# A first-layer product in one-pass float32r parts instead of float32, for the first batch of an attention-then-FFN kernel

## The chip, the cores and the metric

The kernel runs on one core of one Trainium2 chip. The metric is device time in microseconds (us), the median of several executions. Engines are named as the profile names them: PE is TensorE's matrix multiplication, PEld its weight load, DVE is VectorE, ACT is ScalarE, POOL is GpSimd, SP is SyncE, which only issues DMAs here.

## The reference

Eight batches of eight heads, 576 tokens each, 64 values per head. Keys and values are first gathered into 32 memory slots per head by a softmax over the tokens; queries attend to the slots; the result is a matrix of 4608 tokens by 512, which passes two layers of 2048 with h·cos(h) between them.

```python
a = exp(phi - max(phi, over tokens)); a = a / (sum(a, over tokens) + 1e-9)
k_m = einsum('bhsm,bhsd->bhmd', a, k)
v_m = einsum('bhsm,bhsd->bhmd', a, v)
attn = softmax(q @ k_m.T / sqrt(64))          # 32 slots per head
x = attn @ v_m                                 # -> 4608 x 512
h = x @ w_in                                   # 512 -> 2048
out = (h * cos(h)) @ w_out                     # 2048 -> 512
```

The drawn q and k are multiplied by 64 and phi by 3.26, so the softmax is steep. w_in and w_out arrive as float64 and are read as pairs of 32-bit words.

## The kernel before, in words

The values' memory is folded into the first layer: since x = attn @ v_m, the kernel computes v_m @ w_in once per batch (256 rows, that is 8 heads of 32 slots, by 2048) and multiplies the attention weights, transposed into `aT` (two groups of 128 rows by 576 tokens), with these folded weights. The 4608 tokens are cut into 12 groups of 384, and each group passes the 2048 inner columns in 16 steps of 128. One batch has 576 tokens, so a pair of batches makes three groups: 384 tokens of the first, 192 of the first and 192 of the second (`regions`), and 384 of the second.

In step (grp, f) of the main loop `gemm1` makes the first-layer product `hp`, `act` and `act_end` make h·cos(h), and `gemm2` adds to the output's three accumulators, four steps later (`LAG`).

**Precision.** From group 1 on, all large products go as three float16 products of high and low parts: folded weights `vw` and attention `aT` each have a high and a low half, the activations `gp` and the second-layer weights `wo` too. Splitting needs power-of-two scales, which come from the largest weight, and this is known only when all weights have been converted from float64. Group 0 runs while the weights are still arriving. So it uses plain float32: `fold_first(j)` makes folded weights of 256 columns into `vf` (float32, one tile for each quarter of 512 columns), `gemm1` multiplies them with `aTf` (float32, the first 384 tokens), and `gemm2` uses float32 too. Each float32 product is recorded as two matmul rows with a weight load each. The remaining 192 tokens of batch 0 belong to group 1: `back` in `attend(0)` splits them to float16 in `aT`, and `split_first(q)` splits each quarter of `vf` into `vw_0_q` at steps 14, 18, 22 and 26 of the loop (steps count from 0; 16 to a group).

**Order.** The main loop is written by hand: `convert_next` takes one converted block of weights per step in group 0 and calls `fold_first` after each block of w_in; in group 1 each step has one `w_out_split` and one `w_in_split`; the attention of the coming batches is spread over the steps by `jobs`; `fold(b, q)` for batch 1 stands at steps 12, 16, 20 and 24. Within it, the framework's scheduler orders each engine's instructions.

**Buffers that matter.** The tag `vw` has 8 buffers of 4 KB per partition, `aT` has 3 of 4.6 KB, `raw0` to `raw2` have 8 KB each and hold the raw weights, then the parts of `w_in_split`. The float16 copy of w_in for batches from 2 on (`w2`) goes, for quarter q, into the place of quarter q - 1 of `w_in_sb`, and for quarter 0 into `raw0`.

Lines that the steps below touch: L395 and L398 to L401 (`back`: transposes, high part on ACT, low part on DVE), L466 and L467 (`split_fold`), L484 and L486 (`fold_first`: product, copy), L513 and L522 (`gemm1`, float32 and float16), L533 and L536 (`act`, one pair for each region), L541 (the sine), L545, L547 and L548 (`act_end` from group 1 on: times u, high part, low part), L188/L189 and L199/L200 (splits of w_out and w_in in group 1), L143 to L152 (conversion from float64).

Of the kernel before, what the change touches and what calls it, by code (L numbers as in the profile page):

```python
# [8 lines left out]

F16 = mybir.dt.float16  # L10
F32 = mybir.dt.float32
I16 = mybir.dt.int16
I32 = mybir.dt.int32
I8 = mybir.dt.int8
# [3 lines left out]
ALU = mybir.AluOpType  # L18
# [4 lines left out]
P = 128  # L23
# [4 lines left out]
NP = H // 2  # L28
NF = DF // P
FS = 512  # L30
NQ = DF // FS
WS = 256
# [13 lines left out]
def attention_then_ffn(ctx: ExitStack, tc: tile.TileContext, phi, phiT, kv, qT, w_in, w_out, eye, out):  # L46
# [148 lines left out]
    def w_in_split(q, c):  # L195
        if c == 0:
            st["parts"] = ld.tile([P, 2, NP, FS], F16, tag=f"raw{1 + q % 2}", name=f"w_in_parts_{q}")
        parts, s, src = st["parts"], st["s", "in"], w_in_sb[:, c, q * FS:(q + 1) * FS]
        nc.scalar.activation(parts[:, 0, c], src, AF.Copy, scale=s)  # L199
        nc.vector.scalar_tensor_tensor(out=parts[:, 1, c], in0=src, scalar=s, in1=parts[:, 0, c],  # L200
                                       op0=ALU.mult, op1=ALU.subtract)
        if c < NP - 1:
            return
        if q == 0:
            w2 = ld.tile([P, NP, 2, FS], F16, tag="raw0", name="w_in_2_0")
        else:
            w2 = w_in_sb[:, :, (q - 1) * FS:q * FS].bitcast(F16).rearrange("p c (o f) -> p c o f", o=2)
        for o in range(2):
            here, there = slice(o * D, (o + 1) * D), slice((1 - o) * D, (2 - o) * D)
            nc.sync.dma_start(out=w2[here, :, o], in_=parts[here, 0])  # L210
            nc.sync.dma_start(out=w2[there, :, o], in_=parts[here, 1])
        st["w2", q] = w2
# [99 lines left out]
    def scales(b):  # L312
        E = wk.tile([P, 1], F32, tag="E", name=f"E_{b}", bufs=3)
        nc.vector.tensor_scalar(out=E, in0=st["ev", b], scalar1=st["e", "in"], scalar2=None, op0=ALU.mult)
        cu = wk.tile([P, 1], F32, tag="cu", name=f"cu_{b}", bufs=3)
        nc.vector.tensor_scalar(out=cu, in0=E, scalar1=2.0 ** -27 / (2.0 * math.pi), scalar2=None, op0=ALU.mult)
        st["E", b], st["cu", b] = E, cu
        if b < 2:
# [18 lines left out]

    def attend(b):
        qt, km = loads.pop(("q", b)), st["km", b]
        flat = wk.tile([P, 4 * S], F16, tag="aT", name=f"aT_{b}", bufs=3)  # L340

        t32 = GT if b == 0 else 0
        if b == 0:
            st["aTf"] = flat[:, 0:4 * GT].bitcast(F32).rearrange("p (g x) -> p g x", g=2)
        aT = flat[:, 4 * t32:].rearrange("p (w g x) -> p w g x", w=2, g=2)
        st["aT", b] = aT
# [43 lines left out]

        def back(i):
            t0, n = BL[i]
            if t0 < t32:
                for g in range(2):
                    nc.vector.transpose(st["aTf"][:, g, t0:t0 + n], at[:, 2 * t0 + g * n:2 * t0 + (g + 1) * n])  # L395
                return
            bk = wk.tile([P, 2, n], F32, tag="back", name=f"back_{b}_{t0}", bufs=4)
            nc.vector.transpose(bk.rearrange("p g x -> p (g x)"), at[:, 2 * t0:2 * (t0 + n)])  # L398
            c = slice(t0 - t32, t0 + n - t32)
            nc.scalar.mul(aT[:, 0, :, c], bk, 2.0 ** 14)  # L400
            nc.vector.scalar_tensor_tensor(out=aT[:, 1, :, c], in0=bk, scalar=2.0 ** 14, in1=aT[:, 0, :, c],  # L401
                                           op0=ALU.mult, op1=ALU.subtract)
# [65 lines left out]
                                       op0=ALU.mult, op1=ALU.subtract)  # L468

    def fold(b, q):  # L470
        vw = wk.tile([P, 2, 2, FS], F16, tag="vw", name=f"vw_{b}_{q}", bufs=8)
        st["vw", b, q] = vw
        for g, pv in enumerate([fold_psum(b, q, g) for g in range(2)]):
            split_fold(b, vw, g, pv)

    def fold_first(j):
        q, r = divmod(j, 2)
        if r == 0:
            st["vf", q] = wk.tile([P, 2, FS], F32, tag="vw", name=f"vf_{q}", bufs=8)
        pv = small_ps(f"pvf_{j}").rearrange("p (g x) -> p g x", g=2)  # L480
        for g in range(2):
            for i in range(2):
                c = 2 * g + i
                nc.tensor.matmul(pv[D * i:D * (i + 1), g], lhsT=st["vm", 0][:, c],  # L484
                                 rhs=w_in_sb[:, c, j * WS:(j + 1) * WS], start=True, stop=True)
        (nc.scalar.copy if j < 2 else nc.any.tensor_copy)(out=st["vf", q][:, :, r * WS:(r + 1) * WS], in_=pv)  # L486

    def split_first(q):
        vw = wk.tile([P, 2, 2, FS], F16, tag="vw", name=f"vw_0_{q}", bufs=8)
        for g in range(2):  # L490
            split_fold(0, vw, g, st["vf", q][:, g])
        st["vw", 0, q] = vw

    def prep(b):
        yield from memory(b)
# [12 lines left out]
    def gemm1(grp, f):  # L508
        hp = ps_h.tile([P, 512], F32, tag="ps_h", name=f"hp_{grp}_{f}")
        q, fo = divmod(f, FS // P)  # L510
        if grp == 0:
            for g in range(2):
                nc.tensor.matmul(hp[:, :GT], lhsT=st["vf", q][:, g, fo * P:(fo + 1) * P], rhs=st["aTf"][:, g],  # L513
                                 start=(g == 0), stop=(g == 1))
            return hp
        for b, t0, c0, n in regions(grp):
            vw, aT = st["vw", b, q], st["aT", b]
            c1 = t0 if b else t0 - GT
            k = 0
            for g in range(2):  # L520
                for wi, ai in ((0, 0), (0, 1), (1, 0)):
                    nc.tensor.matmul(hp[:, c0:c0 + n], lhsT=vw[:, wi, g, fo * P:(fo + 1) * P],  # L522
                                     rhs=aT[:, ai, g, c1:c1 + n], start=(k == 0), stop=(k == 5))
                    k += 1
        return hp

    def act(grp, f, hp, pin=False):
        u = ew.tile([P, GT], F32, tag="u", name=f"u_{grp}_{f}", bufs=3)
        gp = ew.tile([P, GT], F32, tag="gp", name=f"gp_{grp}_{f}", bufs=6)
        ni = gp.bitcast(I32)  # L530
        for b, t0, c0, n in regions(grp):
            c, cu = slice(c0, c0 + n), st["cu", b] if grp else 1.0 / (2.0 * math.pi)
            ins = nc.scalar.activation(ni[:, c], hp[:, c], AF.Copy, scale=cu, bias=0.25)  # L533
            if pin:
                tc.keep_in_program_order(ins)
            nc.vector.scalar_tensor_tensor(out=u[:, c], in0=hp[:, c], scalar=cu, in1=ni[:, c],  # L536
                                           op0=ALU.mult, op1=ALU.subtract)
        return u, gp

    def act_end(grp, f, hp, u, gp):  # L540
        nc.scalar.activation(u, u, AF.Sin, scale=TWO_PI_BELOW, bias=quarter)  # L541
        if grp == 0:
            nc.vector.tensor_tensor(out=gp, in0=hp[:, :GT], in1=u, op=ALU.mult)
            return grp, f, gp
        nc.vector.scalar_tensor_tensor(out=u, in0=hp[:, :GT], scalar=2.0 ** -17, in1=u, op0=ALU.mult, op1=ALU.mult)  # L545
# [143 lines left out]
    for i in range(12 * NF):  # L689
# [7 lines left out]
            w_out_split(f)  # L697
        if NF <= i < 2 * NF:
            w_in_split((i - NF) // 4, i % 4)
        if i % 4 == 2 and 0 <= i - 14 < 4 * NQ:  # L700
            split_first((i - 14) // 4)
        hp = gemm1(grp, f)
        last = len(pending) == LAG and pending[0][1] == NF - 1
        if last:
# [71 lines left out]
```

## Time and profile before

| | |
|---|---|
| median of 3 runs | 712.89 us (711.32 to 714.12) |
| the profiled execution | 714.09 us, its span 712.3 us |
| mean granted TensorE clock | 0.988 |
| PE busy, whole span | 686.4 us |
| DVE / ACT busy, whole span | 532.4 / 518.7 us |
| first layer of group 0 (L513) | 64 float32 rows, 28.5 to 107.4 us |
| first layer from group 1 on (L522) | 1440 float16 rows, 110.6 to 696.3 us |

The span runs from the first to the last instruction on any engine; the time of an execution adds a little around it. Busy time is the union of an engine's instructions. Matmuls are pipelined: a row lasts longer than the distance to the next, so that distance, and not the row's length, is what a product costs in a sequence. A row of the chain of waits gives a start, a length and the work (engine, tile, line, count) that held up what came after. In a row of groups, "x8 | 5.8, 748 | 3.0 <-ACT" means eight instructions, 5.8 us busy, 748 ns each, and 3.0 us in which the engine stood idle before them, mostly until that ACT instruction was done.

### The profile page before, as it was taken

The numbers are of one execution on the slowest core, as the hardware profiler recorded it, in microseconds if no ns is written. First come the engines' busy times: TensorE is split into PE (matmuls) and PEld (weight loads), VectorE is DVE, ScalarE is ACT, GpSimd is POOL, SyncE is SP. The second block draws the span as 40 slices with busy tenths as digits, with TensorE's granted clock in tenths as the row PEclk, the third lists the DMA queues.
The fourth block names the chain that finished last, engine by engine and source line by source line (L and its number), as shares of the span: only waits on it lengthen the run. The fifth ranks groups of instructions, "written<-read, shape, count | busy, mean of one in ns | idle before, by whom it ended". The sixth has DMA issues, their size and how long they took to land.

```text
span 712.3 us, 11782 instructions
## 1 busy us (share of the span) xinstructions
PE 686.4 (96%) x4578; PEld 364.3 (51%) x4578; DVE 532.4 (75%) x1132; ACT 518.7 (73%) x951; POOL 13.7 (2%) x34
## 2 busy tenths in 40 slices
PE   7689899999999999999999899999999999999997
PEld 3344345556545445566445445666445454665453
DVE  2869879999968966599667885689567976575552
ACT  1799999898875865778766875678767885665652
POOL 0000000000000000000000100000000000000000
PEclk9799999999999999999999999999999999999999
DMA  8996792325507100170104200151100010100101
GB/s 297 379 333 215 237 320 61 104 60 153 186 1 219 60 1 1 46 235 1 44 1 159 84 37 1 46 179 56 44 2 1 9 37 1 46 1 1 45 0 45
DMA packets 32231, 66.77 MB, mean 94 GB/s; under 512 B 2224, under 2 KB 12336, under 8 KB 32176
## 3 DMA queue, kind: packets, MB, share of 16 engines
q1 hardware_dynamic: 27712, 58.02, 25.1%
q10 hardware_dynamic: 4464, 8.00, 2.9%
q8 instruction: 36, 0.59, 0.4%
q14 instruction: 19, 0.16, 0.1%
HBM read 52.38 MB, written 9.44 MB: 87 GB/s over the span
## 4 chain that ended last, share of the span: by engine, by line
PE 63%; DVE 18%; ACT 15%; DMA 2%; issue 1%; SPq 0%; ACTq 0%; DVEq 0%
PE acc L566 35%; PE hp L522 17%; DVE u L536 3%; ACT u L541 3%; DVE u L545 3%; DVE gp L548 2%; PE psA L258 2%; PE hp L513 2%; PE sc L365 2%; DVE vw L467 2%; PE pv L460 2%; ACT gp L547 2%; DVE wo L189 2%; DMA kv<-in_kv 1%; DVE w_in_parts L200 1%
## 5 line engine op out<-in xcount | busy, mean ns | idle before, releaser
L566 PE MATMUL acc<-wo,gp 128*128 128x512 f16 x1584 | 371.9, 379 | 1.4 <-DVE ob L578 0.7
L566 PEld LDWEIGHTS <-gp 128*128 128x128 f16 x1584 | 153.3, 98 | 162.8 <-issue 4.4
L522 PE MATMUL hp<-aT,vw 128*128 128x192 f16 (+1 forms) x1440 | 202.7, 284 | 1.1 <-DVE u L545 1.1
L522 PEld LDWEIGHTS <-vw 128*128 128x128 f16 x1440 | 128.3, 98 | 77.6 <-issue 17.9
L541 ACT ACTIVATE u<-u,quarter 128x384 f32<-128x384 f32 x192 | 117.0, 616 | 64.5 <-DVE u L536 63.6
L545 DVE SCALAR_TENSOR_TENSOR u<-hp,u 128x384 f32<-128x384 f32 x176 | 96.6, 554 | 60.6 <-ACT u L541 60.1
L533 ACT ACTIVATE gp<-hp,cu 128x192 int32<-128x192 f32 (+1 forms) x240 | 115.3, 492 | 27.9 <-PE hp L522 11.8
L536 DVE SCALAR_TENSOR_TENSOR u<-hp,cu,gp 128x192 f32<-128x192 f32 (+1 forms) x240 | 119.0, 504 | 21.9 <-ACT gp L533 21.5
L547 ACT CAST gp<-u 128x384 f16<-128x384 f32 x176 | 88.9, 510 | 55.2 <-DVE u L545 53.9
L548 DVE TENSOR_TENSOR gp<-u,gp 128x384 f16<-128x384 f32 x176 | 96.5, 553 | 43.0 <-ACT gp L547 41.9
L561 PE MATMUL acc<-wo,gp 128*128 128x512 f32 x96 | 45.1, 599 | 0.0
L513 PE MATMUL hp<-aT,vf 128*128 128x384 f32 x64 | 28.2, 579 | 7.3 <-DVE vf L486 3.1
L467 DVE SCALAR_TENSOR_TENSOR vw<-pv,vw 128x512 f16<-128x512 f32 x48 | 31.5, 685 | 3.0 <-ACT vw L466 2.9
L466 ACT ACTIVATE vw<-pv 128x512 f16<-128x512 f32 x48 | 26.8, 588 | 1.1 <-PE pv L460 0.9
L561 PEld LDWEIGHTS acc<-wo,gp 128*128 128x128 f32 x96 | 17.4, 190 | 17.8 <-issue 15.2
L590 ACT ACTIVATE ob<-acc,os 128x512 f32<-128x512 f32 x27 | 17.8, 682 | 9.7 <-PE acc L566 7.1
L258 PE MATMUL psA<-kv,phi 128*32 128x129 f32 (+1 forms) x640 | 21.0, 275 | 3.2 <-DMA kv<-in_kv 1.8
L513 PEld LDWEIGHTS hp<-aT,vf 128*128 128x128 f32 x64 | 13.3, 220 | 20.9 <-issue 5.9
L541 ACT ACT_TABLE_LOAD x17 | 21.8, 1283 | 0.3
L365 PE MATMUL sc<-q,km 128*64 128x256 f32 (+3 forms) x192 | 19.8, 342 | 2.1 <-DVE vw L467 1.7
L258 PEld LDWEIGHTS psA<-kv,phi 128*32 128x32 f32 (+1 forms) x640 | 16.4, 109 | 9.5 <-issue 3.7
L365 PEld LDWEIGHTS sc<-q,km 128*64 128x64 f32 x192 | 12.1, 140 | 12.6 <-issue 4.4
(130 smaller groups left out, 539.7 us busy)
## 6 DMA issues: line engine op xcount, KB each, us to landing
kv<-in_kv SPq DMA_DIRECT2D x32, 516.0 KB, 7.0
raw_out<-in_w_out SPq DMA_DIRECT2D x8, 1024.0 KB, 6.3
q<-in_qT SPq DMA_DIRECT2D x7, 1152.0 KB, 5.5
out<-ob ACTq DMA_DIRECT2D x30, 256.0 KB, 2.1
raw_in<-in_w_in SPq DMA_DIRECT2D x6, 1024.0 KB, 7.6
phi<-in_phi SPq DMA_DIRECT2D x8, 512.0 KB, 6.1
w_in_sb<-w_in_parts SPq DMA_DIRECT2D x12, 256.0 KB, 4.5
phiT<-in_phiT SPq DMA_DIRECT2D x4, 576.0 KB, 9.4
```

The costliest lines, as they stand in the source:

```text
L258: nc.tensor.matmul(psA[32 * j:32 * (j + 1), g * KV:(g + 1) * KV], lhsT=a[:n, c, h * M:(h + 1) * M], rhs=kvs[c][:n, h * KV:(h + 1) * KV], s ...
L365: nc.tensor.matmul(sc[D * p:D * (p + 1), g * n:(g + 1) * n], lhsT=km[:, 2 * g + p], rhs=qt[:, 2 * g + p, t0:t0 + n], start=True, stop=True)
L513: nc.tensor.matmul(hp[:, :GT], lhsT=st["vf", q][:, g, fo * P:(fo + 1) * P], rhs=st["aTf"][:, g], start=(g == 0), stop=(g == 1))
L522: nc.tensor.matmul(hp[:, c0:c0 + n], lhsT=vw[:, wi, g, fo * P:(fo + 1) * P], rhs=aT[:, ai, g, c1:c1 + n], start=(k == 0), stop=(k == 5))
L533: ins = nc.scalar.activation(ni[:, c], hp[:, c], AF.Copy, scale=cu, bias=0.25)
L536: nc.vector.scalar_tensor_tensor(out=u[:, c], in0=hp[:, c], scalar=cu, in1=ni[:, c], op0=ALU.mult, op1=ALU.subtract)
L541: nc.scalar.activation(u, u, AF.Sin, scale=TWO_PI_BELOW, bias=quarter)
L545: nc.vector.scalar_tensor_tensor(out=u, in0=hp[:, :GT], scalar=2.0 ** -17, in1=u, op0=ALU.mult, op1=ALU.mult)
L547: nc.scalar.copy(gp[:, 0], u)
L548: nc.vector.tensor_tensor(out=gp[:, 1], in0=u, in1=gp[:, 0], op=ALU.subtract)
L561: nc.tensor.matmul(accs[grp][t], lhsT=gp[:, t * P:(t + 1) * P], rhs=wo[:, f + 1], start=(f == 0), stop=(f == NF - 1))
L566: nc.tensor.matmul(accs[grp][t], lhsT=gp[:, gi, t * P:(t + 1) * P], rhs=parts[:, wi], start=(f == 0 and gi == 0 and wi == 0), stop=(f == N ...
```

## The change

Batch 0's first layer, in group 0 and in its half of group 1, is made of three products of float32r parts: high times high, low times high, high times low. A float32r tile is written by an engine with float32r as its output type; the low part is the float32 value less that.

```diff
 def back(i):                                   # in attend(b)
-    if t0 < t32:
+    bk = wk.tile([P, 2, n], F32, tag="back", name=f"back_{b}_{t0}", bufs=4)
+    c = slice(t0, t0 + n)
+    if b == 0:
         for g in range(2):
-            nc.vector.transpose(st["aTf"][:, g, t0:t0 + n], at[:, 2 * t0 + g * n:2 * t0 + (g + 1) * n])
+            nc.vector.transpose(bk[:, g], at[:, 2 * t0 + g * n:2 * t0 + (g + 1) * n])
+            nc.scalar.copy(aTr[0][:, g, c], bk[:, g])
+        nc.vector.tensor_tensor(out=aTr[1][:, :, c], in0=bk, in1=aTr[0][:, :, c].bitcast(F32),
+                                op=ALU.subtract)
         return
...
 def fold_first(j):
-        st["vf", q] = wk.tile([P, 2, FS], F32, tag="vw", name=f"vf_{q}", bufs=8)
+        st["vr", q] = [wk.tile([P, 2, FS], F32R, tag="vw", name=f"vr_{q}_{w}", bufs=8) for w in range(2)]
...
-    (nc.scalar.copy if j < 2 else nc.any.tensor_copy)(out=st["vf", q][:, :, r * WS:(r + 1) * WS], in_=pv)
+    high, low = (t[:, :, r * WS:(r + 1) * WS] for t in st["vr", q])
+    nc.scalar.copy(high, pv)
+    nc.vector.tensor_tensor(out=low, in0=pv, in1=high.bitcast(F32), op=ALU.subtract)
-
-def split_first(q):
-    vw = wk.tile([P, 2, 2, FS], F16, tag="vw", name=f"vw_0_{q}", bufs=8)
-    for g in range(2):
-        split_fold(0, vw, g, st["vf", q][:, g])
-    st["vw", 0, q] = vw
...
 def gemm1(grp, f):
-    if grp == 0:
-        for g in range(2):
-            nc.tensor.matmul(hp[:, :GT], lhsT=st["vf", q][:, g, fo * P:(fo + 1) * P], rhs=st["aTf"][:, g],
-                             start=(g == 0), stop=(g == 1))
-        return hp
     for b, t0, c0, n in regions(grp):
+        if b == 0:
+            k = 0
+            for wi, ai in ((0, 0), (1, 0), (0, 1)):
+                for g in range(2):
+                    nc.tensor.matmul(hp[:, c0:c0 + n], lhsT=st["vr", q][wi][:, g, fo * P:(fo + 1) * P],
+                                     rhs=st["aTr"][ai][:, g, t0:t0 + n], start=(k == 0), stop=(k == 5))
+                    k += 1
+            continue
...
 def act_end(grp, f, hp, u, gp):
-    nc.vector.scalar_tensor_tensor(out=u, in0=hp[:, :GT], scalar=2.0 ** -17, in1=u, op0=ALU.mult, op1=ALU.mult)
+    for b, t0, c0, n in [(1, 0, 0, GT)] if grp > 1 else regions(1):
+        c = slice(c0, c0 + n)
+        nc.vector.scalar_tensor_tensor(out=u[:, c], in0=hp[:, c], scalar=2.0 ** -17 if b else st["G"],
+                                       in1=u[:, c], op0=ALU.mult, op1=ALU.mult)
```

What follows from it: batch 0's part of group 1 is no longer scaled to float16's range, so its half of L545 multiplies by a scale `G` of its own, and `act` uses a constant for it. The eight `vr` tiles fill all eight `vw` buffers, so batch 1's first two quarters of folded weights (`vw_1`, 8 KB) move to `raw0`, and the `w2` copy of quarter q now goes into quarter q of `w_in_sb` itself. `aTr` takes two of the three `aT` buffers. The loop no longer calls `split_first`.

More of the change, by code (lines that the diff above doesn't have):

```diff
@@ L11 @@
 F32 = mybir.dt.float32
+F32R = mybir.dt.float32r
 I16 = mybir.dt.int16
@@ L203, in w_in_split @@
             return
[L204 to L207, printed above, removed]
+        w2 = w_in_sb[:, :, q * FS:(q + 1) * FS].bitcast(F16).rearrange("p c (o f) -> p c o f", o=2)
         for o in range(2):
@@ L317, in scales @@
         st["E", b], st["cu", b] = E, cu
-        if b < 2:
+        if b == 0:
+            G = wk.tile([P, 1], F32, tag="G", name="G", bufs=1)
+            nc.vector.reciprocal(out=G, in_=E)
+            nc.vector.tensor_scalar(out=G, in0=G, scalar1=2.0 ** 10, scalar2=None, op0=ALU.mult)
+            st["G"] = G
+        elif b == 1:
             T = wk.tile([P, 1], F32, tag="T", name=f"T_{b}")
@@ L339, in attend @@
         qt, km = loads.pop(("q", b)), st["km", b]
-        flat = wk.tile([P, 4 * S], F16, tag="aT", name=f"aT_{b}", bufs=3)
-        t32 = GT if b == 0 else 0
         if b == 0:
-            st["aTf"] = flat[:, 0:4 * GT].bitcast(F32).rearrange("p (g x) -> p g x", g=2)
-        aT = flat[:, 4 * t32:].rearrange("p (w g x) -> p w g x", w=2, g=2)
-        st["aT", b] = aT
+            st["aTr"] = aTr = [wk.tile([P, 2, S], F32R, tag="aT", name=f"aT_0_{w}", bufs=3) for w in range(2)]
+        else:
+            st["aT", b] = aT = wk.tile([P, 2, 2, S], F16, tag="aT", name=f"aT_{b}", bufs=3)
         at = wk.tile([P, 2 * S], F32, tag="at", name=f"at_{b}", bufs=1)
@@ L470, in fold @@
     def fold(b, q):
-        vw = wk.tile([P, 2, 2, FS], F16, tag="vw", name=f"vw_{b}_{q}", bufs=8)
+        if b == 1 and q < 2:
+            if q == 0:
+                st["vw_1"] = ld.tile([P, 2, 2, 2, FS], F16, tag="raw0", name="vw_1")
+            vw = st["vw_1"][:, q]
+        else:
+            vw = wk.tile([P, 2, 2, FS], F16, tag="vw", name=f"vw_{b}_{q}", bufs=8)
         st["vw", b, q] = vw
@@ L510, in gemm1 @@
         q, fo = divmod(f, FS // P)
-        if grp == 0:
-            for g in range(2):
-                nc.tensor.matmul(hp[:, :GT], lhsT=st["vf", q][:, g, fo * P:(fo + 1) * P], rhs=st["aTf"][:, g],
-                                 start=(g == 0), stop=(g == 1))
-            return hp
-        for b, t0, c0, n in regions(grp):
+        for b, t0, c0, n in regions(grp):
+            if b == 0:
+                k = 0
[5 more added lines that the diff above has]
+                continue
             vw, aT = st["vw", b, q], st["aT", b]
-            c1 = t0 if b else t0 - GT
             k = 0
@@ L522, in gemm1 @@
                     nc.tensor.matmul(hp[:, c0:c0 + n], lhsT=vw[:, wi, g, fo * P:(fo + 1) * P],
-                                     rhs=aT[:, ai, g, c1:c1 + n], start=(k == 0), stop=(k == 5))
+                                     rhs=aT[:, ai, g, t0:t0 + n], start=(k == 0), stop=(k == 5))
                     k += 1
@@ L531, in act @@
         for b, t0, c0, n in regions(grp):
-            c, cu = slice(c0, c0 + n), st["cu", b] if grp else 1.0 / (2.0 * math.pi)
+            c, cu = slice(c0, c0 + n), st["cu", b] if b else 1.0 / (2.0 * math.pi)
             ins = nc.scalar.activation(ni[:, c], hp[:, c], AF.Copy, scale=cu, bias=0.25)
@@ L699, in attention_then_ffn @@
             w_in_split((i - NF) // 4, i % 4)
-        if i % 4 == 2 and 0 <= i - 14 < 4 * NQ:
-            split_first((i - 14) // 4)
         hp = gemm1(grp, f)
```

2 lines of the change are left out of this document (removed).

## The prediction

> **What bounds the kernel now.** I read the page's head first, then a cut of the span into stretches, then the chain of waits inside them, then the groups of instructions and the timeline for durations.
>
> ```profile
> span 712.3 us, 11782 instructions
> PE 686.4 (96%) x4578; PEld 364.3 (51%) x4578; DVE 532.4 (75%) x1132; ACT 518.7 (73%) x951; POOL 13.7 (2%) x34
> ```
>
> TensorE (PE) is busy for 96% of the span, so over the whole kernel it is the bound. The change touches only the work of groups 0 and 1, so the stretches matter: group 0 runs from 28.5 to about 110 us, group 1 to about 168 us. The view by windows gives busy time of PE, PEld, DVE, ACT and POOL, then the granted clock.
>
> ```profile
> 28.50:44.00 15.50, 12.54 (x40) 6.27 (x40) 10.23 (x13) 14.43 (x20) 0.00 (x0) 0.72 1.04 355
> 44.00:78.00 34.00, 31.01 (x192) 15.18 (x188) 31.54 (x64) 32.13 (x45) 0.97 (x3) 1.00 0.72 241
> 78.00:110.00 32.00, 31.87 (x92) 14.99 (x93) 25.57 (x53) 31.15 (x48) 0.74 (x3) 0.95 0.80 269
> 110.00:168.00 58.00, 57.20 (x358) 32.83 (x356) 57.79 (x121) 54.61 (x111) 0.58 (x2) 1.00 0.32 78
> 168.00:712.00 544.00, 535.80 (x3758) 286.65 (x3755) 393.11 (x849) 376.08 (x718) 10.03 (x19) 1.00 0.17 56
> ```
>
> From 168 us on PE alone is full, and the change leaves that work as it is. Before that, three engines are close together. In group 0 ScalarE (ACT) has 14.43 + 32.13 + 31.15 = 77.7 of 81.5 us, so 3.8 us idle; PE has 75.4. In group 1 VectorE (DVE) is busy for 57.79 of 58 us, PE for 57.20, ACT for 54.61. What the change saves on one engine therefore counts only as far as its neighbour gives way. The chain of waits (start, us, what) says who ends last, and its merged rows give the pace of instructions that follow one another.
>
> ```profile
> 28.54 5.46 PE hp L513 x8
> 35.06 0.58 ACT vf L486
> 57.01 1.29 PE hp L513 x4
> 77.50 0.59 DVE vf L486
> 82.70 0.49 ACT gp L533
> 92.45 1.24 DVE w_in_sb L150
> 103.20 1.17 issue
> 104.36 1.30 ACT vw L466 x2
> 112.39 0.52 ACT u L541
> 118.24 1.32 DVE vw L467 x2
> 126.51 0.47 DVE u L545
> 131.53 0.67 DVE u L536 x2
> 174.05 0.97 PE hp L522 x6
> ```
>
> Up to 44 us the chain changes between PE (a half clock: 8 float32 passes in 5.46 us, 0.64 each at first, where later four take 1.29, 0.32 each) and ACT. At 77.50 it is DVE that holds PE, through the copy of folded weights. From 82.70 to 112.39 it is ACT, but for the two long pieces shown between. From 118 us it is DVE almost alone.
>
> **The change part by part.** I take four terms in the order of time, against the profiled execution: 714.09 us, of which 712.3 is span and 1.8 lies around it. That execution is 1.2 above the median of 712.89; I carry the difference over to the median.
>
> First the price of the products, since three of the terms use it. Group 0's first layer is this row: 16 steps of two float32 products over 384 columns, each recorded as two passes.
>
> ```profile
> L513 PE MATMUL hp<-aT,vf 128*128 128x384 f32 x64 | 28.2, 579 | 7.3 <-DVE vf L486 3.1 <-DVE gp L543 2.1 <-DVE aT L395 1.4
> 28.50:44.00 15.50, 8.64 (x16) 3.88 (x16) 0.72 1.04 355
> 44.00:78.00 34.00, 6.13 (x16) 2.79 (x16) 1.00 0.72 241
> 78.00:110.00 32.00, 13.41 (x32) 6.59 (x32) 0.95 0.80 269
> 110.55 1.15 PE L522 MATMUL hp<-aT,vw 128*128 128x192 f16 x12
> L522 PE MATMUL hp<-aT,vw 128*128 128x192 f16 x192 | 18.5, 246 | 0.1
> 55.54 0.61 PE L281 MATMUL tpx<-ident,X 128*128 128x128 f32 x4
> L281 PE MATMUL tpx<-ident,X 128*128 128x128 f32 x4 | 0.6, 274 | 0.0
> ```
>
> By the same line's count in each stretch (time, PE busy with passes in brackets) four steps lie in the first two stretches each and eight in the third. One step costs four passes, 1.29 us. No float32r product is in this trace. Its nearest row by passes is the float16 product over 384 columns, six in 0.97 us (0.162 each); its nearest by bytes is float32 (0.645 for a whole product). I take the former, because both types would go through the array once: a step is then six products, 0.97 us, and 16 steps save 16 x 0.32 = 5.1 us of PE. The Trainium skill, FP8 and Floating Point Precision, section TensorE Precision Notes, says that reduced-precision float32 is read as four bytes and cut to about 22 bits, against four passes for true float32; the two recorded passes at twice the float16 time agree on the four, and no row here shows the other.
>
> In group 1 the first batch has 192 columns a step, six products in float16 before and six in float32r after. The 12 float16 products of the timeline row end 1.15 us after the first begins; less the 0.246 of the last, that is 0.90 for 11, 0.082 each. A float32r product needs a load of four-byte weights. The float32 identity products come with such a load each, four passes in 0.61 us; less 0.274 that is 0.112 a pass, so the load fits into 0.112 us. Over 384 columns 0.162 covers it; over 192 columns 0.082 does not. So the bounds for 96 products are 0.082 (no cost), 0.112 (the load sets the pace: 96 x 0.030 = 2.9 us) and 0.322 (float32's rate, half of 0.645: 96 x 0.240 = 23 us). I take 0.112, the row that shares the kind of load.
>
> ```profile
> L522 PEld LDWEIGHTS <-vw 128*128 128x128 f16 x198 | 16.7, 98 | 7.4 <-issue 4.7 <-ACT u L541 0.2
> L281 PEld LDWEIGHTS tpx<-ident,X 128*128 128x128 f32 x4 | 0.6, 191 | 0.5 <-PE hp L513 0.2 <-issue 0.2
> ```
>
> A four-byte load is recorded at 191 ns, a two-byte one at 98. The Trainium skill, TensorE: Matmul & The Clock Gate, section Weight-path perf modes, says that the fast weight load is on for 128 weights whose type is not FP32. The two durations agree; the page doesn't say on which side float32r falls. If it had the fast load, the 2.9 us would be nothing.
>
> *28.5 to 44 us.* The attention of the first batch must now be split before the first product. DVE transposes as before, into another tile; ACT copies the high parts, four copies of 256 and 128 columns; DVE subtracts 512 and 256 elements.
>
> ```profile
> L400 ACT ACTIVATE aT<-back 128x512 f16<-128x512 f32 x2 | 1.2, 613 | 0.0
> L400 ACT ACTIVATE aT<-back 128x128 f16<-128x128 f32 x1 | 0.3, 293 | 0.0
> L401 DVE SCALAR_TENSOR_TENSOR aT<-back,aT 128x512 f16<-128x512 f32 x2 | 1.4, 676 | 0.0
> L401 DVE SCALAR_TENSOR_TENSOR aT<-back,aT 128x128 f16<-128x128 f32 x1 | 0.3, 285 | 0.0
> 45.70 0.57 ACT L486 COPY vf<-pvf 128x512 f32<-128x512 f32 x1
> L486 DVE COPY vf<-pvf x4: 661/676/680, 48.7 to 96.4; 128x512 f32<-128x512 f32 x4
> 77.41 0.66 DVE L486 COPY vf<-pvf 128x512 f32<-128x512 f32 x1
> 85.94 0.68 DVE L486 COPY vf<-pvf 128x512 f32<-128x512 f32 x1
> ```
>
> Between 293 and 613 ns, 256 columns make about 400: ACT gets 2 x 0.40 + 2 x 0.29 = 1.4 us. DVE gets 0.68 + 0.42, and 0.68 for the low part of the first folded weights: 1.8. DVE has room (10.23 of 15.5), ACT has not (14.43). Against it, PE at half clock needs 12 x 0.32 = 3.9 us instead of 5.46, 1.5 less, but the fold that follows also waits for the conversion of the weights, which passes the same ACT and DVE. I take +1.0; bounds -0.5 and +2.5.
>
> *44 to 78 us.* Each of the eight 256-column folds gets a high copy on ACT and a subtraction on DVE; before, each took one copy, four of them on DVE (the rows above), the first (48.7) and second (77.41) in this stretch, where one fold's copy (45.70) is on ACT already. ACT +2 x 0.58 = 1.2, DVE 3 x 0.68 - 2 x 0.67 = +0.7, and PE -4 x 0.32 = -1.3 for four steps. Block 2 of the attention is split before and after (two copies of 192 for one of 384, +0.2). ACT has 1.87 us idle here, which takes some of it: +0.8; bounds 0 and +2.
>
> *78 to 110 us.* ACT gets two more copies (+1.2) and loses the two split steps of the first quarter of the folded weights (2 x 0.65 = 1.3 by the pace of L466): -0.1; DVE likewise gets 0.7 and loses 2 x 0.66. PE, as full as ACT, loses 2.6 over eight steps. I take -0.6; bounds -2.5 and +1. The second batch's first folded weights go into the buffer of the last raw weights but one. The row below is the end of their conversion; the fold's copy came at 104.36, so 1.0 us covers it. Without that cover the fold slips by the difference, and group 1's first products with it.
>
> ```profile
> 103.07 0.26 ACT L152 ACTIVATION_READ_ACCUMULATOR raw_out<-wo 128x1 f32 x1
> ```
>
> *110 to 168 us.* The other six split steps go: at the paces of the chain DVE loses 6 x 0.66 = 4.0 and ACT 6 x 0.65 = 3.9. But the last multiplication by u (L545) is cut into two halves, one per batch: 2 x 0.33 (a 192-column step, L536) for 0.47, 16 x 0.19 = +3.0. DVE nets -1.0 and, alone, would end the stretch that much earlier. PE, at 57.20 of 58, gets the 2.9 us: 60.1, 2.1 over the stretch if busy were all work. Its busy time holds modelled ends, so I take the middle between -1.0 and +2.1, rounded up: +1.0.
>
> The copies of split weights into place (four DMAs on SP for each quarter) now wait for the fold of their own quarter; that is seven steps earlier in the program, so nothing queued behind them on SP moves. I cost it at nothing; if it were late, the loads of the third batch would wait behind it.
>
> Sum: 1.0 + 0.8 - 0.6 + 1.0 = +2.2 us: 714.09 becomes 716.3, the median 715.1. About 0.5%, 3.6 us, is what a measurement of this kernel can tell from no change, so this is none. The case's own range is 711 to 719.
>
> **The rivals.** Slower: *float32r over 192 columns runs at float32's rate.* For it: no row shows a one-pass product of four-byte operands, and half the columns leave half the time to bring them in. Against: the float32 pass of 128 columns keeps up with its load. Price: 96 x 0.240 = 23 us on PE in group 1. It decides at once, since PE has under 1 us free in that stretch; DVE and ACT then wait. 712.9 + 1.2 + 22 = 736. A milder form, twice the float16 time at 192 columns, costs 96 x 0.08 = 7.7 and gives 720.
>
> Faster: *PE is the real limit in group 0 as well, and ACT's idle time takes its extra.* For it: PE is at 31.87 of 32 us from 78 us on. ACT's 3.8 us idle hold the net extra (1.4 + 1.2 + 0.2 - 0.1 = 2.7). Then PE's 5.1 us come through but for the 1.0 at the start, and group 1 costs nothing: 712.9 - 4.1 - 1.0 = 708. Against: the chain from 82.70 to 112.39 us runs through ACT.
>
> *float32r takes two cycles a column at every width.* Then a step of group 0 costs 6 x 0.32 = 1.93 instead of 1.29, +10 us, with 7.7 in group 1: about 730. That the change saves no pass at all would be still dearer, 16 x 2.6 = 41 us in group 0 alone and some 777.
>
> **How the numbers follow.** The forecast has 0.53, of which 0.41 is within 0.5%, 0.10 slower and 0.02 faster. PE-limited group 0 has 0.13 (0.12 faster, 0.01 same). Float32's rate at 192 columns has 0.20, the milder form 0.07, two cycles everywhere 0.05, anything else 0.02, all slower. Faster is 0.14, same 0.42, slower 0.44. The range goes down to 709, nearly to the faster rival, and up to 737, which takes in the dear one; about 0.17 is left out. The number is that of the likeliest case.
>
> **What would show it.**
>
> ```profile
> L467 DVE SCALAR_TENSOR_TENSOR vw<-vf,T,vw x8: 742/746/758, 108.3 to 152.1; 128x512 f16<-128x512 f32 x8
> ```
>
>  The products at the first layer: about 0.162 us apart over 384 columns and 0.11 over 192. ACT over 28.5 to 110 us busier by about 2.5 us; none of these split steps, which stand between 108.3 and 152.1 now; L545's line twice per step in group 1, about 0.33 each; the first product of group 0 at about 29.3 instead of 28.54. Products 0.3 apart in group 1, or a group 1 of 80 us, would prove the slower rival; a group 0 that ends before 108 us would prove the faster one.

## The result, and the profile after

After the change the kernel takes 733.66 us (median of 4 executions, 731.04 to 734.98), against 713.19 for the kernel before (711.32 to 714.12): a ratio of 1.029, with the interval 1.0268 to 1.0312. The profiled execution of after took 734.98 us, its span 732.9; the span before was 712.3, so 20.6 us are to be found.

The head of the page of after:

```profile
span 732.9 us, 11868 instructions
PE 692.5 (94%) x4610; PEld 376.2 (51%) x4610; DVE 534.9 (73%) x1147; ACT 518.1 (71%) x952; POOL 13.7 (2%) x34
```

No engine has more than 6.1 us more work than before (PE 686.4 to 692.5, DVE 532.4 to 534.9, ACT 518.7 to 518.1), and the span has grown by 20.6. So the time went into waiting. The view by windows of after says in which stretch (time; PE, PEld, DVE, ACT, POOL; granted clock; DMA), first the 80 us from 110 us on, then the whole of group 0:

```profile
110.00:190.00 80.00, 66.86 (x414) 40.05 (x417) 63.21 (x139) 59.52 (x117) 0.66 (x2) 0.94 0.28 66
28.50:110.00 81.50, 71.57 (x351) 41.36 (x348) 69.53 (x133) 78.22 (x115) 1.58 (x5) 0.88 0.81 277
```

and the same two stretches before:

```profile
110.00:190.00 80.00, 78.69 (x548) 44.59 (x546) 78.47 (x173) 71.95 (x142) 1.25 (x4) 1.00 0.45 125
28.50:110.00 81.50, 75.42 (x320) 36.44 (x321) 67.34 (x129) 77.71 (x111) 1.72 (x6) 0.93 0.81 274
```

Before, PE and DVE fill 78.69 and 78.47 of 80 us. After, nobody is full: PE 66.86, DVE 63.21, ACT 59.52. When all engines stand idle in turn, each waits for another, and the chain of waits shows who. Its part for the end of group 1, after ("..." stands for rows left out):

```profile
174.38 0.43 ACT gp L539
174.83 0.43 DVE u L542
175.28 0.62 ACT u L547
175.93 0.69 DVE u L553 x2
176.70 0.52 ACT gp L556
177.24 0.56 DVE gp L557
177.80 0.28 DVE u L542
178.10 0.43 ACT gp L539
...
184.07 1.13 DVE phi L240
186.00 1.05 ACT phi L246
187.09 4.24 PE psA L256 x80
```

One step of `act` and `act_end` is walked through piece by piece, and from one step's L539 to the next 3.72 us pass (174.38 to 178.10). Of another step only the first half of L539 and L542 of the next one comes in between (the row at 177.80): otherwise the steps don't overlap. Sixteen such steps alone are 59.5 us, where group 1 of after takes 75.1 (111.99 to `psA` at 187.09) and group 1 before took 58.9 (110.55 to 169.45). The splits and folds of group 1, which before ran between the pieces of the steps, come on top in part: from 124.90 to 132.58 us the chain of after holds only splits of w_out, L189 on ACT and L190 on DVE in turn, 1.5 us a split. PE's larger waits between 110 and 190 us, after, in us in total, times, longest:

```profile
PE psA L256 <- ACT phi L246: 7.1, 1, 7.1
PE acc L575 <- ACT ob L587: 4.9, 1, 4.9
PE hp L520 <- DVE u L553: 1.2, 2, 1.0
```

and all of them before:

```profile
PE acc L566 <- DVE ob L578: 0.7, 1, 0.7
PE psA L258 <- ACT phi L248: 0.5, 1, 0.5
```

The waits grew by 12.0 us (13.2 against 1.2). The second cause of loss hangs on them. After its 7.1 us of idle time PE runs the 80 products of `psA` in 4.24 us (2.54 before) at a granted clock of 0.58; after the 4.9 us its next nine products of `acc` take 3.72 us in the chain, at 0.54, where nine take 1.94 in the chain of a kernel below in which PE does not stop. That is 1.7 + 1.8 us. The Trainium skill, TensorE: Matmul & The Clock Gate, Part 1 (the HAM clock gate), says that an idle window of about 3.4 us puts the clock back to half and that as long a busy one frees it; both pauses are longer than that, and both rows agree.

The products in float32r, in the view of groups of after (28 to 190 us):

```profile
L520 PE MATMUL hp<-aT,vr 128*128 128x384 f32 x96 | 27.7, 425 | 5.0 <-ACT aT L398 3.0 <-ACT vr L495 1.7
L520 PE MATMUL hp<-aT,vr 128*128 128x192 f32 x96 | 16.3, 306 | 1.2 <-DVE u L553 1.2
L520 PEld LDWEIGHTS hp<-aT,vr 128*128 128x128 f32 x192 | 32.3, 206 | 22.6 <-issue 5.6 <-ACT aT L398 3.8 <-ACT vr L495 2.8
```

192 products have 192 records, where a float32 product had two. What a step costs is seen in the timeline. After, six float32r products over 192 columns, then six in float16 for the other half of the step, then nine of the second layer:

```profile
160.05 2.11 PE L575 MATMUL acc<-wo,gp 128*128 128x512 f16 x9
161.80 1.00 PE L520 MATMUL hp<-aT,vr 128*128 128x192 f32 x6
162.64 0.67 PE L528 MATMUL hp<-aT,vw 128*128 128x192 f16 x6
163.15 2.11 PE L575 MATMUL acc<-wo,gp 128*128 128x512 f16 x9
```

and before, all twelve in float16:

```profile
132.68 1.17 PE L522 MATMUL hp<-aT,vw 128*128 128x192 f16 x12
133.68 2.11 PE L566 MATMUL acc<-wo,gp 128*128 128x512 f16 x9
135.63 1.15 PE L522 MATMUL hp<-aT,vw 128*128 128x192 f16 x12
```

From start to start the float32r six take 0.84 us here (0.75 to 1.05 over the steps of group 1) and the float16 six 0.51. But the first float32r product is recorded early: it starts 1.75 us after the first of the nine second-layer products (160.05 to 161.80), the first float16 one 1.95 us after (133.68 to 135.63). So the price is the distance from step to step. Where PE doesn't stand, that is 3.10 us after (160.05 to 163.15) and 2.95 before (132.68 to 135.63; 2.93 in later steps): six float32r products cost 0.15 to 0.17 us more than six in float16, and 16 steps 2.4 to 2.7 us.

With group 1's first product 1.4 us later (110.55 to 111.99) the parts are 1.4 + 12.0 + 1.7 + 1.8 and 2.4 to 2.7 us, together 19.3 to 19.6 for 20.6; about 1 us is not placed. From the end of group 1 on after keeps its distance: the `psA` of the fourth batch begins at 234.85 us against 214.11, that of the eighth at 563.66 against 544.49.

### The profile page after: what moved, and what is told of

Read it like the earlier page. It is cut to its first block, busy times and chain, and to the rows that moved or that the text cites. A ratio compares the mean times of both kernels' runs of the same rounds, so it can differ in the third digit from the quotient of the medians.

```text
span 732.9 us, 11868 instructions
## 1 busy us (share of the span) xinstructions
PE 692.5 (94%) x4610; PEld 376.2 (51%) x4610; DVE 534.9 (73%) x1147; ACT 518.1 (71%) x952; POOL 13.7 (2%) x34
## 4 chain that ended last, share of the span: by engine, by line
PE 60%; ACT 20%; DVE 13%; DMA 4%; issue 1%; SPq 1%; ACTq 0%; DVEq 0%
PE acc L575 34%; PE hp L528 17%; ACT u L547 4%; DVE u L553 3%; PE psA L256 2%; DVE u L542 2%; DVE gp L557 2%; ACT gp L556 2%; PE pv L463 2%; ACT gp L539 2%; PE sc L365 2%; DMA kv<-in_kv 1%; ACT L547 1%; ACT wo L146 1%; DVE vw L470 1%
## 5 line engine op out<-in xcount | busy, mean ns | idle before, releaser
L528 PE MATMUL hp<-aT,vw 128*128 128x192 f16 (+1 forms) x1344 | 194.7, 286 | 2.2 <-DVE u L553 2.2
L547 ACT ACTIVATE u<-u,quarter 128x384 f32<-128x384 f32 x192 | 116.5, 613 | 68.7 <-DVE u L542 68.0
L528 PEld LDWEIGHTS <-vw 128*128 128x128 f16 x1344 | 119.2, 98 | 72.4 <-issue 14.8
L553 DVE SCALAR_TENSOR_TENSOR u<-hp,u 128x384 f32<-128x384 f32 (+1 forms) x176 | 93.4, 535 | 60.8 <-ACT u L547 60.2
L539 ACT ACTIVATE gp<-hp,cu 128x192 int32<-128x192 f32 (+1 forms) x224 | 109.1, 497 | 33.8 <-DVE u L542 17.4
L542 DVE SCALAR_TENSOR_TENSOR u<-hp,cu,gp 128x192 f32<-128x192 f32 (+1 forms) x224 | 112.7, 511 | 24.5 <-ACT gp L539 24.1
L556 ACT CAST gp<-u 128x384 f16<-128x384 f32 x176 | 88.6, 509 | 59.0 <-DVE u L553 57.9
L557 DVE TENSOR_TENSOR gp<-u,gp 128x384 f16<-128x384 f32 x176 | 96.5, 553 | 45.8 <-ACT gp L556 44.8
L570 PE MATMUL acc<-wo,gp 128*128 128x512 f32 x96 | 48.5, 630 | 3.7 <-DVE wo L151 3.7
L520 PE MATMUL hp<-aT,vr 128*128 128x384 f32 (+1 forms) x192 | 44.0, 365 | 6.3 <-ACT aT L398 3.0
L520 PEld LDWEIGHTS hp<-aT,vr 128*128 128x128 f32 x192 | 32.3, 206 | 22.6 <-issue 5.6
L256 PE MATMUL psA<-kv,phi 128*32 128x129 f32 (+1 forms) x640 | 22.7, 290 | 10.1 <-ACT phi L246 7.1
L463 PE MATMUL pv<-w_in_sb,vp 128*32 128x512 f16 x192 | 19.4, 384 | 0.0
```

The source lines that it names most:

```text
L256: nc.tensor.matmul(psA[32 * j:32 * (j + 1), g * KV:(g + 1) * KV], lhsT=a[:n, c, h * M:(h + 1) * M], rhs=kvs[c][:n, h * KV:(h + 1) * KV], s ...
L520: nc.tensor.matmul(hp[:, c0:c0 + n], lhsT=st["vr", q][wi][:, g, fo * P:(fo + 1) * P], rhs=st["aTr"][ai][:, g, t0:t0 + n], start=(k == 0), ...
L570: nc.tensor.matmul(accs[grp][t], lhsT=gp[:, t * P:(t + 1) * P], rhs=wo[:, f + 1], start=(f == 0), stop=(f == NF - 1))
```

## The experiments

**What was to be told apart.** Theory A: the framework's scheduler, which fixes each engine's order when the kernel is built, takes a float32r product of under 256 columns for far dearer than it is. It then finds no use in mixing the steps, and writes group 1's ACT and DVE queues strictly one step after another. The rivals: the products themselves are slow (the slower rival of the prediction), the moved buffers delay the transfers, group 0's added steps make everything late. The order of each queue is fixed when the kernel is built, and the traces list it. ACT's, for steps 9 to 11 of group 1 (gp b0 and b1 are L539 of the two halves, sine is L547, cast is L556):

```
after:  gp 9 b0 | gp 9 b1 | sine 9 | cast 9 | gp 10 b0 | gp 10 b1 | split | sine 10 | split | split | cast 10 | gp 11 b0
256:    gp 10 b0 | sine 9 | gp 10 b1 | cast 9 | sine 10 | gp 11 b0 | split | cast 10 | gp 11 b1 | split | gp 12 b0 | sine 11
before: gp 10 b0 | split | sine 9 | gp 10 b1 | cast 9 | sine 10 | gp 11 b0
```

In after, step 10 begins only when ACT's part of step 9 is over, and so it goes from step 8 to the last (a few earlier steps overlap); the other two have two steps under way.

**Wider products: 256 and 240 columns.** Group 1's float32r products are computed over 256 (then 240) columns, of which 192 are used. To make room, both halves of a step stand in other columns of `hp`, in both kernels alike; all else is as after. This gives PE more to do, not less.

```diff
-    nc.tensor.matmul(hp[:, c0:c0 + n], lhsT=..., rhs=st["aTr"][ai][:, g, t0:t0 + n], ...)
+    m = max(n, 256)                       # 240 in the second kernel
+    o = slice(512 - m, 512) if m > n else slice(c0, c0 + n)
+    nc.tensor.matmul(hp[:, o], lhsT=..., rhs=st["aTr"][ai][:, g, t0 + n - m:t0 + n], ...)
```

> First batch's half of group 1 as float32r products over 256 columns, 64 of them surplus, in another place of the PSUM tile. Theory A (the scheduler that orders the queues prices a float32r product under 256 columns far above its cost, and orders ACT and DVE for a slow PE): the order becomes that of float16, group 1 steps overlap again, 712 to 717 us, though PE works no less: about 0.115 us a product. Theory B (the products themselves are dear): at least 733. Theory C (moved buffers: the w2 copies wait for folds and hold up the splits): 728 to 734. Theory D (the later first product, 32.1 for 28.5 us): no change, 733.

> The same with 240 columns in place of 256. Theory A, if the scheduler's bound lies at 256: 730 to 735, with PE work equal to that of the 256 columns within 1 us. Theories B, C, D: the same as with 256 columns, within 2 us.

Measured: 717.73 us with 256 columns (715.09 to 720.98), 1.006 of before [1.0039, 1.0081]; 735.02 with 240 (734.89 to 735.59), 1.0299 [1.0278, 1.032]. Sixteen columns more take 17.3 us off. The ranges of theory A, 712 to 717 and 730 to 735, are missed by 0.7 us and just met. From 133.5 us to the end of group 1 the chain of waits with 256 columns is PE alone (here L527 is the float32r product, L535 float16, L583 the second layer):

```profile
153.55 0.70 PE hp L527 x6
154.25 0.51 PE hp L535 x6
154.76 1.94 PE acc L583 x9
156.71 0.71 PE hp L527 x6
```

3.16 us a step. With 240 columns it is the serial chain of after, piece for piece (L547, L550, L555, L561, L564, L565 are after's L539, L542, L547, L553, L556, L557):

```profile
170.86 0.43 ACT gp L547
171.31 0.43 DVE u L550
171.76 0.62 ACT u L555
172.41 0.69 DVE u L561 x2
173.18 0.52 ACT gp L564
173.72 0.56 DVE gp L565
174.28 0.28 DVE u L550
174.59 0.43 ACT gp L547
```

3.73 us a step, and the same two long waits (7.0 us ahead of `psA`, 5.3 ahead of `acc`). The busy time of 60 us of group 1, first with 256, then with 240 columns:

```profile
110.00:170.00 60.00, 58.13 (x342) 35.46 (x341) 56.35 (x133) 50.77 (x104) 0.66 (x2) 1.00 0.33 76
```

```profile
110.00:170.00 60.00, 52.05 (x288) 29.89 (x287) 50.00 (x112) 45.07 (x89) 0.66 (x2) 0.94 0.28 68
```

The products themselves lie 0.117 to 0.120 us apart at 256 columns, 0.114 at 240 and 0.113 at 192 (distances between the starts of single records): nothing jumps at 256. What jumps is the order of the instructions. Of theory A this much held: the order turns with the width, and the time with the order. Products at float32's rate are out. That the scheduler's price of the product is the reason is inferred: its prices were not read, only that width alone turns the order.

**Float16 products in group 1.** Both halves of group 1 use batch 1's float16 parts (so batch 0's 192 tokens are computed from other data of the same shapes); group 0 as after.

```diff
-    return [(b0, GT, 0, S - GT), (b0 + 1, 0, S - GT, S - GT)]
+    return [(b0 if pair else 1, GT, 0, S - GT), (b0 + 1, 0, S - GT, S - GT)]
```

> The first batch's half of group 1 is computed with the second batch's float16 parts in place of its own (that half of the output is another batch's), all else as after the change. Theory A: 711 to 716, about 3 less than with 256 columns, since PE saves 96 x 0.03 us. Theory B: below 716 as well. Theory C: 728 or more, as the buffers stay moved. Theory D: 730 or more.

Measured: 716.42 us, 1.0048 [1.0029, 1.0068]. Without float32r in group 1 the 20 us are gone too, with group 0's changes all in place (theory A's range, 711 to 716, is missed by 0.4). What is left is 3.7 us.

**The buffers alone.** The kernel before, with `w2` of each quarter in its own quarter of `w_in_sb` and batch 1's first folded weights in `raw0`.

```diff
-        if q == 0:
-            w2 = ld.tile([P, NP, 2, FS], F16, tag="raw0", name="w_in_2_0")
-        else:
-            w2 = w_in_sb[:, :, (q - 1) * FS:q * FS]...
+        w2 = w_in_sb[:, :, q * FS:(q + 1) * FS]...
...
-        vw = wk.tile([P, 2, 2, FS], F16, tag="vw", name=f"vw_{b}_{q}", bufs=8)
+        if b == 1 and q < 2:
+            if q == 0:
+                st["vw_1"] = ld.tile([P, 2, 2, 2, FS], F16, tag="raw0", name="vw_1")
+            vw = st["vw_1"][:, q]
+        else:
+            vw = wk.tile([P, 2, 2, FS], F16, tag="vw", name=f"vw_{b}_{q}", bufs=8)
```

> The kernel before with the moved buffers alone: w2 of a quarter into its own quarter of w_in_sb, the second batch's first two folded quarters into raw0. Theory A, B, D: 712 to 714, no change. Theory C: 725 or more.

Measured: 713.43 us, 1.0001 [0.9984, 1.0018]. In the order of the kernel before, the moves cost nothing. That isn't shown for the other orders. In the kernel with 256 columns the chain runs through a copy of `w2` into `w_in_sb`, the tile that the fold of batch 1 (L457) reads, and PE waits 1.9 us for it:

```profile
126.73 6.53 DMA w_in_sb<-w_in_parts
133.50 1.94 PE pv L457 x8
```

With float16 in group 1 PE waits 2.0 us at the same place; the kernel before and this one don't have that wait. In after a copy of 5.08 us into `w_in_sb`, from 143.55, stands in the chain ahead of a split of w_in (L200). So some of what stays in those kernels can be the moved buffers'; no kernel here has the change without the moves.

**What remains.** With the order mended (256 columns) 5.0 us stay. In its profile they are not group 0's: group 1's first product comes at 107.58 us, 3.0 earlier than before, and then the wider products cost 3.16 us a step for 2.93 to 2.95, which is 3.4 to 3.7 us over 16 steps, and the copy into `w_in_sb` 1.9. But this execution, of 715.09 us, was the fastest of ten. Four kernels on that one: only the high times high products in group 0 (the other two parts of each product left out); the two transposed blocks first, one high copy for each, then the subtractions; the high copies of the folds from the third on moved to DVE; and the last two edits together.

```diff
 high only:
-                for wi, ai in ((0, 0), (1, 0), (0, 1)):
+                for wi, ai in ((0, 0), (1, 0), (0, 1)) if grp else ((0, 0),):
 order of back:
-                for i in p:
-                    back(i)
+                parts = [back(i) for i in p]
+                for bk, c in parts:
+                    nc.scalar.copy(aTr[0][:, :, c], bk)
+                for bk, c in parts:
+                    nc.vector.tensor_tensor(out=aTr[1][:, :, c], in0=bk, ...)
 high copies on DVE:
-        nc.scalar.copy(high, pv)
+        (nc.scalar.copy if j < 2 else nc.vector.tensor_copy)(high, pv)
```

> On top of the 256 columns (717.7 us): group 0 makes only the product of high and high parts, two float32r products a step instead of six (its outputs are then of lower precision); the low parts are still made. PE loses 16 x 4 x 0.175 = 11 us in group 0. Theory E (ACT bounds group 0, so PE time saved there doesn't arrive): 714 to 718. Theory F (PE bounds group 0): 706 to 709.

> On top of the 256 columns: the first batch's attention is transposed in both blocks first, then copied to high parts (one copy for each block instead of two), then subtracted. ACT loses about 0.4 us and the first product comes about 0.7 us earlier. If the start is on the path: 716 to 717; if ACT's total bounds group 0: about 0.4 less than 717.7; if neither: no change.

> On top of the 256 columns: the high copies of the folded weights from the third on move from ACT to DVE, six copies: ACT loses 6 x 0.58 = 3.5 us in group 0, DVE gets 6 x 0.67 = 4.0. Theory E: 714 to 716. Theory F: no change, or up to 2 slower where DVE holds PE.

> Both of these edits. Theory E: 713 to 715.5, at or just above the kernel before (712.7). Theory F: 717 to 719.

Measured: 717.84 [1.0048, 1.0092], 718.69 [1.006, 1.0103], 720.82 [1.0091, 1.0133] and 719.79 [1.0077, 1.0121], against 717.73 without any of them. Group 0 with 256 columns, and then with the high products alone:

```profile
28.50:110.00 81.50, 74.98 (x366) 44.24 (x367) 70.63 (x135) 80.49 (x118) 1.57 (x5) 0.90 0.78 273
```

```profile
28.50:110.00 81.50, 64.66 (x291) 31.74 (x292) 68.70 (x133) 77.87 (x115) 1.64 (x5) 0.86 0.78 273
```

PE does 10.3 us less in the second, and the time is the same, as theory E has it: these products saved in group 0 are worth nothing. Neither is ACT's load alone the answer: taking six copies off ACT made it slower by 3.1 us, which neither theory had; the order of `back` changed nothing that can be told apart, and both edits together came out above both ranges. The edits move more than their own pieces: with the high products alone group 1's first product comes at 113.30 us, 5.7 later than with all six.

**Group 0 apart from group 1.** Three kernels with float16 in group 1 as above: L553 whole again (one piece of 384 columns); that, and no low parts in group 0 (the high parts stand in for them; ten subtractions and the tiles of the low parts are left out); and the kernel before, with only batch 1's parts in group 1's first half and `split_first` gone.

```diff
 whole (on the float16 kernel):
-        for b, t0, c0, n in [(1, 0, 0, GT)] if grp > 1 else regions(1):
+        for b, t0, c0, n in [(1, 0, 0, GT)]:
 no low parts (on "whole"):
-                nc.vector.tensor_tensor(out=aTr[1][:, :, c], in0=bk, in1=aTr[0][:, :, c].bitcast(F32),
-                                        op=ALU.subtract)
...
-        nc.vector.tensor_tensor(out=low, in0=pv, in1=high.bitcast(F32), op=ALU.subtract)
 old group 0 (on the kernel before):
-            return [(b0, GT, 0, S - GT), (b0 + 1, 0, S - GT, S - GT)]
+            return [(b0 if pair else 1, GT, 0, S - GT), (b0 + 1, 0, S - GT, S - GT)]
...
-        if i % 4 == 2 and 0 <= i - 14 < 4 * NQ:
-            split_first((i - 14) // 4)
```

> The float16 stand-in of group 1 (second batch's parts, 716.4 us) with the multiplication by u in one piece of 384 columns, as before the change: DVE loses 16 x 0.19 = 3.0 us in group 1. What is left over the kernel before is group 0's part alone, less the split steps that the change removes. Theory G (the halves of that multiplication hold the rest): 713 to 714. Theory H (group 0 holds it): 715.5 to 716.5.

> The same without any low parts in group 0: the high part stands in for them, so products and copies stay and ten subtractions on DVE go (outputs of the first 384 tokens are of lower precision). DVE loses about 7 us in group 0. Theory H1 (it is the subtractions, and what waits for them): 712 to 713.5. Theory H2 (it is the copies on ACT and the start): within 1 us of the run with low parts.

> The kernel before with the second batch's float16 parts in place of the first's in group 1 and without the split steps of folded weights: group 0 as before, group 1 as in the run with the multiplication in one piece. Theory H: 709 to 712, 4 or more below that run, since DVE loses 8 x 0.66 and ACT 8 x 0.61 us. Theory G: equal to that run within 1 us, 713.

Measured: 718.78, 1.0089 [1.0056, 1.0122]; 719.82, 1.0086 [1.0057, 1.0116]; 713.49, 1.0009 [0.9985, 1.0033]. The first lies above the ranges of both theories, the second fits H2, the third is 5.3 us below the first, as H has it, but above H's range. The halves of L553 cost nothing that can be measured. The split steps of the folded weights, which the change removes, are worth nothing that can be measured either: without them the kernel with its old group 0 is no faster than before. From the third to the first of the three only group 0 and its buffers differ in the program, and this makes 5.3 us. It isn't the subtractions alone.

Where these 5.3 us are lost is another matter. The profiled execution of the first took its median, 718.78 us. Its group 1 begins at 109.70 us, against 110.33 with the old group 0, and the third batch's `psA` at 169.18 against 168.61. The loss comes in group 2, whose program is the same in both but for the place of buffers. PE's first-layer products there, first with L553 whole, then with the old group 0:

```profile
199.61 3.94 PE L528 MATMUL hp<-aT,vw 128*128 128x384 f16 x15 [2.73 <-DVE u L553]
195.12 2.92 PE L522 MATMUL hp<-aT,vw 128*128 128x384 f16 x17 [1.24 <-DVE u L545]
```

PE stands for 2.73 us ahead of the one and for 1.24 ahead of the other, and then 15 products take longer than 17: the granted clock from 200 to 210 us is 0.83 in the first and 1.00 in the second. At the fourth batch's `psA` the first is 5.6 us late (219.72 against 214.14). At the end the two executions are 2.8 us apart: the second waits near 400 us, and it took 716.26 us, 2.8 above its median. So in these two executions the loss, too, is a wait far behind the steps that were changed.

**Float32 products, with the copies kept.** The kernel with L553 whole, but group 0 multiplies the high parts in two float32 products a step instead of six in float32r; all copies and subtractions stay.

```diff
-                for wi, ai in ((0, 0), (1, 0), (0, 1)):
-                    for g in range(2):
-                        nc.tensor.matmul(hp[:, c0:c0 + n], lhsT=st["vr", q][wi][...], rhs=st["aTr"][ai][...], ...)
+                for g in range(2):
+                    nc.tensor.matmul(hp[:, c0:c0 + n], lhsT=st["vr", q][0][...].bitcast(F32),
+                                     rhs=st["aTr"][0][...].bitcast(F32), start=(g == 0), stop=(g == 1))
```

> The stand-in with the multiplication in one piece (718.8 us), with group 0's six float32r products replaced by two float32 products that read the same high parts; every copy and subtraction of group 0 stays (the low parts are made and not read). PE gains 16 x 0.24 = 3.8 us of work. Theory I (the added steps of group 0 on ACT and DVE make the 5 us over the run with the old group 0, 713.5): 718 to 721. Theory J (the float32r products do, by their weight loads or by the queue order that goes with them): 713 to 715.

Measured: 719.13, 1.0094 [1.007, 1.0118], as with float32r (718.78) and in theory I's range. But equal times don't show one cause here: with float32 group 1's first product comes at 112.40 us, 2.7 later than with float32r, and the two lose their time at different places. PE's waits up to 112 us show what the added steps do in group 0. With float32r (L553 whole), the two largest:

```profile
PE acc L570 <- DVE wo L151: 3.7, 2, 3.1
PE hp L520 <- ACT aT L398: 3.0, 1, 3.0
```

and with the old group 0, the three largest (with float32 and the copies the same two waits are 3.8 and 3.0 us):

```profile
PE hp L513 <- DVE vf L486: 2.8, 1, 2.8
PE hp L513 <- DVE gp L543: 2.1, 1, 2.1
PE hp L513 <- DVE aT L395: 1.4, 1, 1.4
```

The wait for the attention doubles, from 1.4 to 3.0 us: its high copy on ACT now stands before the first product. And a wait of 3.7 us that the old group 0 doesn't have at all is for the conversion of w_out (L151). Against these stand the waits of 2.8 and 2.1 us that it has alone. The conversions share ACT and DVE with the added steps, and their last piece on ACT ends at 112.05 and 112.63 us in the two kernels, at 109.16 with the old group 0 and at 114.81 in after. That these late conversions are the 5 us is not shown, and the profile with L553 whole speaks against it: its group 1 isn't late. No kernel took the attention's copies and the folds' copies away one by one, and none changed group 0 and kept the order of the rest. What the 5.3 us are stays open. No kernel here was faster than the one before.

## Why the prediction was right and wrong

The forecast was 715.1, no change that can be measured; the kernel came out at 733.66, inside the range of 709 to 737 only because the range took in the slower rival. That is luck: the rival's mechanism is not what happened. The likeliest case was wrong, and one step of it failed.

**The step that failed: 110 to 168 us, +1.0.** It added up the busy time that each engine gains and loses and asked which of three full engines would be full last. That takes for granted that the order of the work stays as it was. The built kernel of after has another order, in which most steps of group 1 end before the next begins. Then the length of a step is the sum of its pieces on ACT and DVE, 3.72 us, the splits no longer run beside them, and the busy time of no engine gives the length of the stretch. PE's waits grew by 12.0 us and the clock that fell after them took 3.5 more, where the step had +1.0. The stretch's sums could not have shown this; the order of ACT's instructions does. That order has a second effect: the softmax of the third batch (L240, L246) queues behind that chain, and PE stands for 7.1 us ahead of `psA`; the output's evacuation (L587) stands on ACT behind three splits of w_in (1.93 us of the chain before it), and PE stands for 4.9 us.

**The price of a product, 192 columns: right.** 0.112 was forecast from the identity products' loads, 0.113 us was measured. The load, too, is that of four-byte weights: 190 ns in the median (206 in the mean, row L520 PEld) against 191 for float32's and 98 for float16's. The Trainium skill, TensorE: Matmul & The Clock Gate, Weight-path perf modes, leaves the fast load to types other than FP32; by this row float32r is on FP32's side. From step to step 96 products cost 2.4 to 2.7 us; 2.9 was forecast.

**The price over 384 columns: a little too low.** 0.162 was forecast, 0.175 measured from product to product. Six of them make 1.05 us where four float32 passes made 1.29: in after the six second-layer products of two steps begin at 106.18 and 109.81 us, 3.63 apart, before at 103.88 and 107.74, 3.86 apart. So a step saves 0.23 to 0.24 us of PE and not 0.32, and 16 steps 3.8 and not 5.1; PE's busy time over group 0 fell by 3.85 (75.42 to 71.57). The kernel with only high products shows that 10 more would have bought nothing.

**Group 0: +1.0, +0.8 and -0.6, together +1.2.** In the profiled execution group 1's first product comes 1.4 us later, which looks right. It is luck: the same group 0 brings it at 107.58 us in the kernel with 256 columns and at 109.77 in the one with float16, both earlier than the 110.55 before. The start was underrated: the first product of group 0 came at 32.1 us, not at 29.3. The added steps were named and priced rightly (a high copy of 577 ns and a subtraction of 679 in the mean of after, forecast 0.58 and 0.68; ACT +2.8 us of busy time with 256 columns, forecast 2.5, though only +0.5 in after). By the medians the kernel with the new group 0 is 5.3 us slower than with the old one, but in its profile group 0 ends on time and the loss lies in group 2. So whether PE's saving pays for the added steps within group 0 stays open; that the whole time would follow group 0's sum is what failed.

**The split steps' 4.0 us on DVE and the halves' 3.0: both nothing.** Taking the split steps out alone moved the time by 0.0009 [-0.0015, 0.0033]; making the halves whole again did not help. With the queues interleaved, PE sets the pace of group 1, as the chain with 256 columns shows.

**The moved buffers and copies, put at nothing: right in the order of before,** at 1.0001. In the kernels with 256 columns and with float16 in group 1 PE waits 1.9 and 2.0 us for such a copy.

**The rivals.** The slower rival had the place, the sign and nearly the time (736), by a mechanism that is refuted: its products would lie 0.322 us apart and lie 0.113 apart. Its second sign, a group 1 of 80 us, was almost there (75.1 us from 111.99 to `psA` at 187.09) and proved nothing by itself; the distance between products did. Nor would the sign of the faster rival have proved it: with 256 columns group 0 ends before 108 us, and the kernel is slower than before. That float32r takes two cycles everywhere falls with the same rows. The faster rival, PE as group 0's limit, has the kernel of high products alone against it: 10.3 us of PE's work less, and no time gained.

## What to carry to other kernels

A scheduler that fixes the queues at build time can answer a change of one operand's type or width with another order for every engine; compare the order of the instructions before and after, and only then add up prices. When no engine is full, look in the chain of waits for a step that is walked through without any other step's work between, and test it by a change that turns the order and gives the engines no less work. Before saving work on one engine, take the work away altogether once and see whether the time moves. And when an edit brings a few microseconds, look where in the profile they are lost: here 5 us that came with an edit of group 0 were lost in group 2.

## What the hardware showed that was not expected

- float32r products lie 0.113 us apart over 192 columns, 0.114 over 240, 0.117 to 0.120 over 256 and 0.175 over 384: from 192 to 256 columns width hardly counts, and no threshold shows. The float16 product of 192 columns takes 0.085 (0.51 for six). In sequence six float32r products over 384 columns take 1.05 us, four float32 passes 1.29.
- Nine second-layer products take 1.94 us where PE doesn't stop and 3.72 after a pause of 4.9, at a granted clock of 0.54: that pause cost nearly 2 us more than its own length.
